# A transformer layer in FP32: right operands of the first FFN block made in reverse order, their sums a tile earlier, and another order of steps where the first attention ends

## The chip, the cores and the metric

The kernel runs on one core of one Trainium2 chip. The metric is the device time of one execution in microseconds (us). A core has these engines, each with a queue of its own that is worked off in order: PE (TensorE, matrix products; loading a stationary operand into it is listed apart as PEld), DVE (VectorE), ACT (ScalarE), POOL (GpSimd), and SP (SyncE), which here only issues DMAs. Matmul results land in PSUM banks, from which DVE and ACT read them; everything else lies in SBUF. Semaphores tie the engines together.

## The reference

One layer on 2048 rows of 576: attention with 32 query heads of 18 columns and one key/value head, then a bilinear feed-forward net (FFN) with 4608 hidden columns, each with a layernorm ahead of it and a residual sum behind it, all in FP32.

```python
q = (x @ wq).reshape(B, S, 32, 18);  k = x @ wk;  v = x @ wv
p = softmax(einsum("bhqd,bkd->bhqk", q, k) * 18 ** -0.5)
h = x + einsum("bhqk,bkd->bhqd", p, v).reshape(B, S, 576) @ wo     # x normalised ahead of q, k, v
g = n @ w_gate;  u = n @ w_up                                      # n: h normalised
out = h + (g * u) @ w_down
```

## The kernel before

**Blocks and tiles.** The 2048 rows are four blocks of 512 (b = 0 to 3). Matrix products keep FP32's accuracy by splitting an operand into a rounded part, hi (a cast), and the rest, lo (a difference, source minus hi), and summing three products: hi hi, hi lo, lo hi. `split` (line 86) does this with a copy on ACT, DVE or POOL and the difference on DVE (line 89).

**Attention** is done in pairs. `pair` (456) issues, for two heads and 128 keys, the scores on PE (`s`, line 476) and the exponential on ACT (`P`, 477). Two pairs make one step of `acc` (481), the product with the values, which `flush` (484) issues later. 32 pairs make a head group of four heads; eight groups make a block, so 256 pairs a block and 1024 in all. With a group's last step DVE transposes `acc` into `os` (492), and a step is put on the list `aux`: `normalise` (506), which divides by the sums, transposes back (523 to 528) and spreads the heads' rows over `ob` with DMAs (537). When enough heads are there, `chunk` splits their rows, and `project` (590) multiplies them with `wo` on PE (`yo`, 605) and adds the result to the residual on DVE (606). `run_aux` (496) takes due steps off `aux`, by default one a call; a call is a round.

**The order is written out by hand.** Block b+1's attention runs inside block b's FFN. Ahead of that, `blocks` (936) ends the first block's attention: first the splits of `wo` (until pair WO_FROM = 228), then the flag, then pairs and projections in turn, in which `fill` (864) issues about one pair for each 1.05 us that it is given. Then comes the layernorm: `normal` (631) makes `xh` on DVE and POOL, and `spread` (641) transposes it on PE (`tx`, 654) and splits it into `X`. It takes the pairs as far as a count that leaves 4 when divided by 8, and four more.

**The flag** (372) tells whether a bound on the scores is passed anywhere; if so, everything is computed a second time at the end with exact maxima. It takes a maximum on DVE, transposes it on PE (379) and compares on DVE.

**FFN.** `ffn` (791) goes through 36 tiles f of 128 hidden columns. A tile has 27 steps j, each with one matmul for `pg` and one for `pu` (811); while attention is left, a pair is issued at every fourth j and one behind the last, 8 a tile. ACT copies `pg` to `g` (835) and DVE multiplies `pu` by it, `hf` (839), which frees the PSUM banks of `pg` and `pu` for the next tile and, in even tiles, for `down`. Weights come by `load_w` (DMA `wr`) and `split_w` (POOL casts, DVE subtracts, `ws`), a tile ahead. Two tiles make a pair of halves p (0 to 17), which `down` (717) multiplies with `w_down` at the end of the next even tile: 42 matmuls `y` (771), using seven right operands in the order 0, 3, 4, 2, 5, 6, 1 (`ORDER`, 1032); this is a Strassen-like scheme with seven products in place of eight. DVE (774) or ACT and POOL (778, 779, over five buffers `tmp`) add the results to the residual.

**Right operands.** In block 0 they are made: `load_raw` (882) brings the four quarters of `w_down` for p, `right_sums` (889) makes three sums on POOL (891), `right` (902) makes one more sum (914), and for each operand a cast on POOL (915), a difference on DVE (918) and a DMA to HBM (921), from where blocks 1 to 3 load them. All these tiles have the tag `wdo`, ten buffers used in turn, as many as one p needs: two raw, one for sums, seven operands. Both run in odd tiles: the sums at j = 4, an operand at every odd j from 7 on. The last p (17) has no sums and four plain operands.

Of the kernel before, what the change touches and what calls it, by code (L numbers as in the profile page):

```python
# [17 lines left out]
F32 = mybir.dt.float32  # L18
# [7 lines left out]
P = 128  # L26
# [5 lines left out]
NG = H // 4  # L32
NF = F // P
NC = NF // 2
HT = TB // 2
HD = D // 2
# [22 lines left out]
class Block:  # L59
# [424 lines left out]
    def flush(self, n):  # L484

        for b, g, t, Ps in self.pend[:n]:
            if t == 0:
                self.acc = self.ps_a(f"acc{b}_{g}")
            self.values(self.acc, Ps, t)
            if t == NT - 1:  # L490
                os_ = self.os[g] = self.op.tile([P, TB], F32, tag="os", bufs=1, name=f"os{b}_{g}")
                self.dve.transpose(os_, self.acc)
                self.aux.append((self.round + 1, lambda b=b, g=g, o=os_: self.normalise(b, g, o), None))
        del self.pend[:n]

    def run_aux(self, limit=1, within=False):
# [93 lines left out]
    def project(self, b, c):  # L590

        pe, dve = self.pe, self.dve
        h, to = self.h[b], self.heads_to(b, c)
        w = self.wos.pop(c) if b else self.wo_0[0:rows(b, c), :, c]
        for s in range(NQ):
            sl = slice(s * P, (s + 1) * P)
            for n in range(2):
                y = self.ps_y(2 * s + n, f"yo{b}_{c}_{s}_{n}")
                d = slice(n * HD, (n + 1) * HD)
                if c < 4 or b == 0:  # L600
                    ms = [(to[0][:, sl], w[:, 0, d]), (to[1][:, sl], w[:, 0, d]), (to[0][:, sl], w[:, 1, d])]
                else:
                    ms = [(to[0][:, sl], w[:, 0, d]), (to[0][:, sl], w[:, 1, d])]
                for i, (m, k) in enumerate(ms):
                    pe.matmul(y[:, :HD], m, k, start=(i == 0), stop=(i == len(ms) - 1))  # L605
                dve.tensor_tensor(h[:, s, d], h[:, s, d], y[:, :HD], ALU.add)
            if b == 0:
                if c == 4:
                    self.statistics(b, s)
                if s % 2:  # L610
                    self.fill(2.4)
        if c == 3 and b:
            self.aux.append((self.round, lambda: self.chunk(b, 4), None))
        if c == 4:
            if b == 0:
                self.normed[b] = self.mv, self.rstd(self.mv[:, :, 1], f"b{b}")
            else:
                self.aux.append((self.round, lambda: self.all_statistics(b), None))
# [172 lines left out]
    def ffn(self, b):  # L791
        pe, act, dve = self.pe, self.act, self.dve
        X, hid, todo = self.X, [], None
        for f in range(NF):
            n_ = NF * b + f
            k = f % 2
            w = self.ws.pop(n_)
            on = self.more(b + 2)
            last = f == NF - 1 and b + 1 < NB
            if on:  # L800
                pg, pu = self.ps_f(f"pg{n_}"), self.ps_f(f"pu{n_}")
            else:
                gu = self.ps_s(f"gu{n_}")
                pg, pu = gu[:, 0], gu[:, 1]
            j = 0
            for c in range(9):
                for wk, xk in ((0, 0), (0, 1), (1, 0)):
                    if on and not last and j % 4 == 0 and self.more(b + 2):
                        self.pair()
                    for o, ps in ((0, pg), (64, pu)):  # L810
                        pe.matmul(ps, w[o:o + 64, wk, c], X[o:o + 64, xk, c], start=(j == 0), stop=(j == 26))  # L811
                    if j == (8 if on else 2) and todo and not plain(n_ - 2):
                        self.left_sums()
                    if j == 3:
                        self.split_w(n_ + 1)
                    if j == 5 and k:
                        self.left_first(n_ - 1, hid[0])
                    if j == 12:
                        self.run_aux(within=True)
                    if b == 0 and k and self.first:  # L820
                        if j == 4:
                            self.right_sums(f // 2)
                            parts = self.right(f // 2)
                        elif j > 6 and j % 2:
                            next(parts, None)
                    if j == 21 and b == f == 0:
                        self.flush(len(self.pend))
                    if j == 6 and last:
                        self.normal(b + 1)
                    j += 1  # L830
            if todo and not on:
                drain(self.down(b, *todo))
                self.more_wd(b, 7)
            g = self.hh.tile([P, TB], F32, tag="g", bufs=1, name=f"g{n_}")
            act.copy(g, pg)  # L835
            if on and not last and self.more(b + 2):
                self.pair()
            hf = self.hh.tile([P, TB], F32, tag="hf", bufs=2, name=f"hf{n_}")
            dve.tensor_tensor(hf, pu, g, ALU.mult)  # L839
            hid.append(hf)  # L840
            if k:
                self.left(n_ - 1, hid)
                hid = []
            self.flush(len(self.pend))
            if todo and on:
                drain(self.down(b, *todo))
                self.more_wd(b, 7)
            if f < NF - 1:
                self.run_aux()
            todo = (f // 2,) if k else None  # L850
        if b + 1 < NB:
            both(self.spread(b + 1), self.down(b, *todo))
            self.more_wd(b + 1, WD_BUFS if b == 0 and self.first else 4)
            if b + 2 < NB:
                self.load_x(b + 2)
        else:
            drain(self.down(b, *todo))
# [31 lines left out]
    def right_sums(self, p):  # L889

        sub = lambda o, x, y: self.nc.gpsimd.tensor_tensor(o, x, y, ALU.subtract)
        a, b = self.raw
        s = self.src = {0: a[:, 0], 1: a[:, 1], 2: b[:, 0], 3: b[:, 1]}
        if p == NC - 1:
            return
        r = self.wp.tile([P, 2, HD], F32, tag="wdo", bufs=WD_BUFS, name=f"sums{p}")
        s[4], s[5], s[6], s[7] = r[:, 0], r[:, 1], s.pop(0), r[:, 0]
        sub(s[4], s[6], s[1])
        sub(s[5], s[3], s[4])
        sub(s[6], s[3], s[6])  # L900

    def right(self, p):

        pool, dve, sp = self.nc.gpsimd, self.dve, self.sp
        s, ws, order = self.src, {}, range(4) if p == NC - 1 else ORDER
        o = 0 if p == NC - 1 else 1
        steps = list(order)
        self.raw = None
        for k in range(len(steps) + 2):
            if k < len(steps):  # L910
                j = steps[k]
                w = ws[j] = self.wdo[0, p, j] = self.wp.tile([P, 2, HD], F32R, tag="wdo", bufs=WD_BUFS, name=f"wdo0_{p}_{j}")
                if o and j == 6:
                    pool.tensor_tensor(s[7], s[2], s[5], ALU.subtract)
                pool.tensor_copy(w[:, 0], s[j + o])  # L915
            if 0 < k <= len(steps):
                j = steps[k - 1]
                dve.tensor_tensor(ws[j][:, 1], s[j + o], f32(ws[j][:, 0]), ALU.subtract)  # L918
            if k > 1:
                j = steps[k - 2]  # L920
                sp.dma_start(self.wd_dram[p, :, j], f32(ws.pop(j)))
            yield
        del s
        self.src = None
        self.load_raw(p + 1)
# [10 lines left out]
    def blocks(self):  # L936

        work = self.load_wo_0()
        self.steps(lambda: self.n_pair < WO_FROM, work)
        drain(work)  # L940
        self.wo_from = WO_FROM + 12
        if self.first:
            work = self.flag()
            self.steps(lambda: self.n_pair < WO_FROM + 8, work)
            drain(work)
        self.cast = self.dve.tensor_copy
        self.steps(lambda: self.more(0))
        self.cast = self.act.copy
        self.load_w(0)
        self.load_w(1)  # L950
        self.fill(2.0, 1)
        while 0 not in self.normed:
            self.run_aux(1)
            self.fill(1.0, 1)
        self.split_w(0)
        while self.n_pair % 8 != 4:
            self.pair()
            if not self.half:
# [73 lines left out]
ORDER = (0, 3, 4, 2, 5, 6, 1)  # L1032
WD_BUFS = 10
LANDING = 6
WO_FROM = 228
# [15 lines left out]
def plain(n):  # L1051

    return n % NF == NF - 2
# [6 lines left out]
def f32(ap):  # L1060
    return ap.bitcast(F32)
# [10 lines left out]
def rows(b, c):  # L1072

    return 7 * DH if b == 0 and c < 4 else P


def drain(gen):
    for _ in gen:
        pass
# [78 lines left out]
```

## Time and profile before

| | |
|---|---|
| median of 3 runs | 2346.53 us (2346.36 to 2346.98) |
| the profiled execution | 2345.53 us |
| its span, first to last instruction | 2343.7 us |
| TensorE clock granted, mean over the span | 0.995 |
| PE / PEld / DVE / ACT / POOL busy | 98% / 69% / 52% / 61% / 29% |
| chain that ended last, by engine | PE 88%, DVE 4%, POOL 3%, issue 2%, ACT 1%, DMA 1% |

The profile is of one execution. A row of a timeline has the start in us from the span's start, the duration in us (from the first to the end of the last where `xN` are merged), engine, operation, tiles written <- read, shapes, and in brackets the engine's idle time ahead of it with what ended it. A row of groups has count, busy time in us, mean ns of one, then idle time ahead and its releasers. A row of stretches has the busy time in us of PE, PEld, DVE, ACT and POOL with the number of instructions, then the granted clock, the share of the DMA engines and GB/s. Rows of the chain have start, duration, engine, tile and line. A matmul's duration overlaps its neighbour's, so PE is read by distances between starts.

### The profile page before, as it was taken

The page shows a single profiled execution, that of the slowest core. Times are in us where ns is not written, and L with a number is a line of the kernel's source. Part 1 is how long each engine was busy: PE and PEld are TensorE (multiplying, and loading weights), DVE is VectorE, ACT ScalarE, POOL GpSimd, SP SyncE. Part 2 cuts the span into 40 slices and gives each one's busy share as a digit, 9 for nine tenths or more (in the row PEclk, how much of TensorE's full clock was granted, in tenths as well). Part 3 has the DMA queues.
Part 4 walks back from the last instruction along what each step waited for, and adds up shares of the span by engine and source line. Part 5 has one row for each costly group of instructions (what it writes and reads, how often), then busy time and mean ns, then how long its engine had stood idle before and what let it go on. Part 6 is the DMA issues. An engine that isn't in the chain of part 4 may idle for free.

```text
span 2343.7 us, 46343 instructions
## 1 busy us (share of the span) xinstructions
PE 2292.6 (98%) x18225; PEld 1605.7 (69%) x18225; DVE 1207.9 (52%) x2174; ACT 1431.9 (61%) x1869; POOL 673.1 (29%) x873
## 2 busy tenths in 40 slices
PE   5999999999999999999999999999999999999998
PEld 4344434676767667777767767767777788888887
DVE  7333334566656566444444445534444476555665
ACT  4888876766666766567676767567676623223332
POOL 3100000455444345222222212312222234333332
PEclk9999999999999999999999999999999999999999
DMA  4222222443334443633433333544333345655553
GB/s 142 70 65 84 72 79 72 145 148 130 126 117 143 142 137 134 205 127 122 127 118 108 117 118 122 154 157 123 114 122 119 111 145 190 203 183 176 168 179 117
DMA packets 127225, 306.59 MB, mean 131 GB/s; under 512 B 15679, under 2 KB 16447, under 8 KB 126999
## 3 DMA queue, kind: packets, MB, share of 16 engines
q1 hardware_dynamic: 126999, 303.54, 39.9%
q8 instruction: 146, 2.39, 0.4%
q14 instruction: 80, 0.66, 0.1%
HBM read 234.00 MB, written 55.67 MB: 124 GB/s over the span
## 4 chain that ended last, share of the span: by engine, by line
PE 88%; DVE 4%; POOL 3%; issue 2%; ACT 1%; DMA 1%; SPq 0%; POOLq 0%; ACTq 0%; DVEq 0%
PE acc L481 19%; PE y L771 16%; PE pg L811 13%; PE s L476 12%; PE gu L811 12%; PE pu L811 10%; PE yo L605 3%; PE psq L331 3%; POOL wdo L915 1%; DVE wdo L918 1%; PE y L729 1%; ACT P L477 1%; POOL ws L88 0%; POOL x L779 0%; DVE hf L839 0%
## 5 line engine op out<-in xcount | busy, mean ns | idle before, releaser
L477 ACT ACTIVATE P<-s 128x1024 f32<-128x1024 f32 x1024 | 1024.6, 1027 | 291.0 <-PE s L476 211.6
L811 PE MATMUL pu<-X,ws 64*128 64x512 f32 x2565 | 699.8, 391 | 4.1 <-DVE hf L839 4.1
L811 PE MATMUL pg<-X,ws 64*128 64x512 f32 x2565 | 701.5, 391 | 0.0
L811 PEld LDWEIGHTS pg<-X,ws 64*128 64x128 f32 x2565 | 475.8, 186 | 53.6 <-DMA wr<-in_wgu_dram 0.8
L811 PEld LDWEIGHTS pu<-X,ws 64*128 64x128 f32 x2565 | 472.8, 186 | 46.2 <-DVE hf L839 7.1
L481 PE MATMUL acc<-P,V 128*32 128x512 f32 x4096 | 492.2, 600 | 1.1 <-ACT P L477 0.6
L476 PE MATMUL s<-q,kT 56*128 56x512 f32 x2048 | 443.0, 424 | 4.0 <-ACT P L477 3.3
L771 PEld LDWEIGHTS y<-wdo,room 128*128 128x128 f32 x2856 | 386.6, 188 | 52.8 <-issue 42.5
L771 PE MATMUL y<-wdo,room 128*128 128x288 f32 x2856 | 407.2, 301 | 2.3 <-DVE h L774 2.3
L778 ACT COPY tmp<-y 128x288 f32<-128x288 f32 x408 | 162.9, 400 | 328.8 <-PE y L771 323.8
L476 PEld LDWEIGHTS s<-q,kT 56*128 56x128 f32 x2048 | 198.3, 185 | 207.0 <-ACT P L477 119.8
L779 POOL TENSOR_TENSOR x<-x,tmp 128x288 f32<-128x288 f32 x204 | 159.2, 811 | 568.6 <-ACT tmp L778 566.9
L811 PE MATMUL gu<-X,ws 64*128 64x512 f32 x2646 | 308.1, 389 | 0.2
L811 PEld LDWEIGHTS gu<-X,ws 64*128 64x128 f32 x2646 | 256.0, 184 | 45.7 <-issue 4.0
L481 PEld LDWEIGHTS acc<-P,V 128*32 128x32 f32 x4096 | 114.5, 109 | 250.1 <-issue 233.0
L88 POOL CAST ws<-wr 128x1152 fp32r<-128x1152 f32 x144 | 169.1, 1174 | 354.9 <-PE gu L811 110.2
L779 POOL TENSOR_TENSOR h<-h,tmp 128x288 f32<-128x288 f32 x204 | 159.4, 812 | 341.7 <-ACT tmp L778 341.1
L89 DVE TENSOR_TENSOR ws<-wr,ws 128x1152 fp32r<-128x1152 f32 x144 | 204.2, 1418 | 77.5 <-POOL ws L88 77.5
L839 DVE TENSOR_TENSOR hf<-pu,g 128x512 f32<-128x512 f32 x95 | 65.5, 690 | 269.7 <-ACT g L835 269.7
L774 DVE TENSOR_TENSOR x<-x,y 128x288 f32<-128x288 f32 x272 | 117.4, 453 | 153.1 <-PE y L771 153.1
L774 DVE TENSOR_TENSOR h<-h,y 128x288 f32<-128x288 f32 x272 | 117.4, 453 | 93.0 <-PE y L771 90.2
L89 DVE TENSOR_TENSOR room<-S,room 128x1024 fp32r<-128x1024 f32 x68 | 83.3, 1225 | 132.3 <-ACT room L88 132.3
(169 smaller groups left out, 1729.3 us busy)
## 6 DMA issues: line engine op xcount, KB each, us to landing
wdo<-wd_dram SPq DMA_DIRECT2D x369, 288.0 KB
wr<-in_wgu_dram SPq DMA_DIRECT2D x144, 576.0 KB
wd_dram<-wdo SPq DMA_DIRECT2D x123, 288.0 KB
q<-q_dram SPq DMA_DIRECT2D x64, 216.0 KB
raw<-in_wd_dram SPq DMA_DIRECT2D x36, 288.0 KB
q_dram<-qs SPq DMA_DIRECT2D x16, 504.0 KB
X<-X SPq DMA_DIRECT2D x28, 256.0 KB
x<-in_x_dram SPq DMA_DIRECT2D x16, 288.0 KB
```

What stands on the lines that cost most here:

```text
L88: (copy or self.cast)(hi, src)
L89: self.dve.tensor_tensor(lo, src, f32(hi), ALU.subtract)
L331: pe.matmul(ps[:r], w[o:o + 64], m[o:o + 64], start=(k == 0), stop=(k == 13))
L476: self.pe.matmul(s_[:, i], self.kT[o:o + 56, t * P:(t + 1) * P], q[o:o + 56, pr], start=True, stop=True)
L477: self.act.activation(p_, s_, AF.Exp, scale=SCALE)
L481: self.pe.matmul(acc[32 * j:32 * j + 32, :], self.V[:, t, :], Ps[j // 2][:, j % 2, :], start=(t == 0), stop=(t == NT - 1), skip_group_chec ...
L605: pe.matmul(y[:, :HD], m, k, start=(i == 0), stop=(i == len(ms) - 1))
L771: pe.matmul(y[:, :HD], m[:, t * P:(t + 1) * P], k, start=(first and j == 0), stop=(j == 2), skip_group_check=True)
L774: dve.tensor_tensor(hs, hs, y[:, :HD], ALU.add)
L778: act.copy(z, y[:, :HD])
L779: pool.tensor_tensor(hs, hs, z, ALU.add)
L811: pe.matmul(ps, w[o:o + 64, wk, c], X[o:o + 64, xk, c], start=(j == 0), stop=(j == 26))
```

## The change

In `flush`, block 0's last group is normalised at once instead of through `aux`. In `project`, `fill` gets 2.1 instead of 2.4. In `blocks`, projections may begin at pair WO_FROM + 8 instead of + 12, the flag's steps are gone, the first two weight loads come at pair 228 and the first weight split ahead of the end of the pairs, and `run_aux` may take two steps a round while it waits for the layernorm. In `ffn`, block 0's even tiles make the three sums (one at each odd j from 9 on), its odd tiles make the operands from j = 7 on as before, and the flag's two parts stand in tiles 2 and 3 at j = 16. The operands are made in the order 1, 5, 2, 6, 4, 3, 0 (the last p, 17, with its plain ones: 3, 2, 1, 0), and the fourth sum is written over a raw quarter instead of over the first sum.

```diff
@@ flush
-                self.aux.append((self.round + 1, lambda b=b, g=g, o=os_: self.normalise(b, g, o), None))
+                if b == 0 and g == NG - 1:
+                    self.normalise(b, g, os_)
+                else:
+                    self.aux.append((self.round + 1, lambda b=b, g=g, o=os_: self.normalise(b, g, o), None))
@@ project
-                    self.fill(2.4)
+                    self.fill(2.1)
@@ ffn
-                    if b == 0 and k and self.first:
-                        if j == 4:
-                            self.right_sums(f // 2)
-                            parts = self.right(f // 2)
-                        elif j > 6 and j % 2:
+                    if b == 0 and self.first:
+                        if j == (6 if k else 8):
+                            parts = self.right(f // 2) if k else self.right_sums(f // 2)
+                        if j % 2 and j > (6 if k else 8):
                             next(parts, None)
+                        if j == 16 and f in (2, 3):
+                            flag = self.flag() if f == 2 else flag
+                            next(flag, None)
@@ right_sums
-        if p == NC - 1:
-            return
-        r = self.wp.tile([P, 2, HD], F32, tag="wdo", bufs=WD_BUFS, name=f"sums{p}")
-        s[4], s[5], s[6], s[7] = r[:, 0], r[:, 1], s.pop(0), r[:, 0]
-        sub(s[4], s[6], s[1])
-        sub(s[5], s[3], s[4])
-        sub(s[6], s[3], s[6])
+        self.raw = None
+        if p < NC - 1:
+            r = self.wp.tile([P, 2, HD], F32, tag="wdo", bufs=WD_BUFS, name=f"sums{p}")
+            s[4], s[5], s[6], s[7] = r[:, 0], r[:, 1], s.pop(0), s[2]
+            for i, x, y in ((4, 6, 1), (5, 3, 4), (6, 3, 6)):
+                sub(s[i], s[x], s[y])
+                yield
@@ right
-        s, ws, order = self.src, {}, range(4) if p == NC - 1 else ORDER
-        o = 0 if p == NC - 1 else 1
-        steps = list(order)
-        self.raw = None
+        s, ws, o = self.src, {}, int(p < NC - 1)
+        steps = (1, 5, 2, 6, 4, 3, 0) if o else (3, 2, 1, 0)
@@ blocks
-        self.wo_from = WO_FROM + 12
-        if self.first:
-            work = self.flag()
-            self.steps(lambda: self.n_pair < WO_FROM + 8, work)
-            drain(work)
+        self.wo_from = WO_FROM + 8
+        self.load_w(0)
+        self.load_w(1)
         self.cast = self.dve.tensor_copy
+        self.steps(lambda: self.n_pair < WO_FROM + 8)
+        self.split_w(0)
         self.steps(lambda: self.more(0))
         self.cast = self.act.copy
-        self.load_w(0)
-        self.load_w(1)
         self.fill(2.0, 1)
         while 0 not in self.normed:
-            self.run_aux(1)
+            self.run_aux(2)
             self.fill(1.0, 1)
-        self.split_w(0)
```

## The prediction

> **What bounds the kernel now.** I read the page first, then the busy times of three stretches of equal meaning, then the chain of waits.
>
> ```profile
> span 2343.7 us, 46343 instructions
> PE 2292.6 (98%) x18225; PEld 1605.7 (69%) x18225; DVE 1207.9 (52%) x2174; ACT 1431.9 (61%) x1869; POOL 673.1 (29%) x873
> ...
> core 0: us, PE busy (x) PEld busy (x) DVE busy (x) ACT busy (x) POOL busy (x), PEclk, DMA share, GB/s
> 323.20:402.05 78.85, 71.63 (x462) 32.89 (x463) 38.20 (x94) 53.73 (x58) 6.76 (x9) 0.96 0.16 46
> ...
> 439.50:944.90 505.40, 500.44 (x4052) 354.25 (x4048) 312.40 (x531) 338.51 (x437) 237.27 (x309) 1.00 0.40 136
> 1004.05:1496.40 492.35, 492.15 (x4052) 350.22 (x4048) 227.68 (x419) 339.36 (x437) 115.70 (x133) 1.00 0.38 120
> ...
> 500.90 6.11 PE y L771 x42
> ...
> 1037.23 5.83 PE y L771 x42
> 1066.91 5.82 PE y L771 x42
> ```
>
> TensorE sets the time, so only what makes it wait or run slowly can be won. Two places have such time. The end of the first attention (323 to 402 us) leaves it idle for 78.85 - 71.63 = 7.2 us and at 0.96 of its clock. FFN block 0 (its 16 downs from 439.5 to 944.9) does the same 4052 matmuls as block 1 does from 1004.05 to 1496.40, in 505.40 instead of 492.35 us: 13.05 us more. Block 0 differs by making the right operands on POOL and DVE. The chain gives one part: a down's 42 matmuls take 6.11 us there and 5.83 in block 1, 0.28 x 16 = 4.5 us. The other 8.6 lie in the tiles, and the timeline of one pair of tiles shows where:
>
> ```profile
> 477.28 0.82 POOL L891 TENSOR_TENSOR sums<-raw 128x288 f32<-128x288 f32 x1
> 478.18 1.80 POOL L891 TENSOR_TENSOR sums<-raw,sums 128x288 f32<-128x288 f32 x1
> 479.95 0.99 POOL L891 TENSOR_TENSOR raw<-raw,raw 128x288 f32<-128x288 f32 x1
> 480.88 0.43 POOL L915 CAST wdo<-raw 128x288 fp32r<-128x288 f32 x1
> ...
> 481.34 0.65 DVE L918 TENSOR_TENSOR wdo<-raw,wdo 128x288 fp32r<-128x288 f32 x1 [1.07 <-POOL wdo L915]
> ...
> 482.51 0.39 DVE L523 TENSOR_SCALAR rc<-os 128x16 f32<-128x16 f32 x1
> ...
> 485.00 1.38 DVE L918 TENSOR_TENSOR wdo<-sums,wdo 128x288 fp32r<-128x288 f32 x1
> ...
> 487.87 0.44 DVE L918 TENSOR_TENSOR wdo<-raw,wdo 128x288 fp32r<-128x288 f32 x1
> 488.24 0.67 DVE L839 TENSOR_TENSOR hf<-pu,g 128x512 f32<-128x512 f32 x1
> ...
> 483.95 0.58 ACT L835 COPY g<-pg 128x512 f32<-128x512 f32 x1
> 488.97 0.50 PE L811 MATMUL pu<-X,ws 64*128 64x512 f32 x1 [0.80 <-DVE hf L839]
> ```
>
> This is tile 5. POOL's three sums hold its casts up until 480.88, DVE waits 1.07 us for the first cast, then works without a break, with the normalise of a head group in between (482.5 to 485.0), until hf at 488.24, though g was there at 484.53. PE needs hf, since it frees pu's bank, and stands still. So the chain of this place is POOL sums, POOL casts, DVE differences, hf, PE.
>
> **The change, part by part.** *The flag leaves the attention.* These are PE's rows about it:
>
> ```profile
> 321.61 1.07 PE L481 MATMUL acc<-P,V 128*32 128x512 f32 x8
> ...
> 325.62 1.07 PE L481 MATMUL acc<-P,V 128*32 128x512 f32 x8
> 328.99 0.20 PE L379 MATMUL psx<-C,mx 32*1 32x32 f32 x1 [2.30 <-DVE mx L376]
> 329.12 1.22 PE L476 MATMUL s<-q,kT 56*128 56x512 f32 x4
> 330.28 1.94 PE L481 MATMUL acc<-P,V 128*32 128x512 f32 x8
> ...
> 338.17 1.87 PE L605 MATMUL yo<-wo,oT 126*128 126x288 f32 x12
> ...
> 320.00:340.00 20.00, 16.78 (x99) 5.56 (x91) 8.97 (x16) 14.41 (x16) 5.83 (x6) 0.83 0.42 134
> ```
>
> Four pairs take 4.01 us (321.61 to 325.62). The eight from 325.62 to the first project at 338.17 take 12.55 instead of 8.0: 4.5 us for the flag, of which 2.30 is the wait of its transpose for DVE's maximum and the rest matmuls at a lower granted clock (0.83 in this slice; eight acc records 1.94 us instead of 1.07). In the tiles the maximum stands a whole tile ahead of its transpose, so nothing waits; PE pays the 0.20 us matmul and a weight load, DVE three small operations in tiles with slack. I put 0.3 us there (bounds 0.2, the matmul alone, and 2.5, the same wait again).
>
> [...]
>
> *Projections from pair 236 instead of 240, normalise of the last group at once, two aux steps a round, fill 2.1.* I counted the order on PE along the code (S one pair, A one acc step, Y one s of a project). Between the first and the fourth project before and after both have 12 Y, 22 S and 12 A, so the 31.40 us from 338.17 to 369.57 stay. The first project begins four pairs earlier and without the flag: 12.55 becomes 4.0, minus 8.5 us. From the fourth project to the first gate matmul it was YYSSYYSSASSAA, YYSSSYYSASSAASSAASS, then transposes and SSAA; it becomes YYSSYYSSAS, YYSASYYSASSAAASS and the same end, four pairs fewer.
>
> ```profile
> 369.57 1.45 PE L605 MATMUL yo<-wo,oT 126*128 126x288 f32 x9
> 371.32 0.67 PE L605 MATMUL yo<-wo,oT 126*128 126x288 f32 x3 [0.30 <-DVE x L606]
> 380.03 1.74 PE L605 MATMUL yo<-wo,oT 128*128 128x288 f32 x11 [0.31 <-DVE oT L89]
> 394.82 2.40 PE L654 MATMUL tx<-C,xh 128*128 128x128 f32 x20 [0.94 <-ACT P L477]
> ...
> 365.40 0.72 DVE L492 STREAM_TRANSPOSE os<-acc 128x512 f32<-128x512 f32 x1 [2.09 <-PE acc L481]
> ...
> 390.28 1.36 DVE L89 TENSOR_TENSOR ws<-wr,ws 128x1152 fp32r<-128x1152 f32 x1
> ...
> L477 ACT ACTIVATE P<-s 128x1024 f32<-128x1024 f32 x280 | 272.3, 1024 | 72.1 <-PE s L476 71.2 <-ACT P L477 0.3
> ...
> 2184.64 0.69 DVE L839 TENSOR_TENSOR hf<-gu,g 128x512 f32<-128x512 f32 x1 [3.37 <-ACT g L835]
> 2202.93 0.69 DVE L839 TENSOR_TENSOR hf<-gu,g 128x512 f32<-128x512 f32 x1 [3.36 <-ACT g L835]
> ```
>
> Leg one (9.8 us, to the fifth project at 379.35) loses S, A, A = 2.2 us of PE work, but DVE's transpose (0.72) and normalise (about 1.7) now stand directly ahead of the fourth project's adds, so the wait of 0.30 becomes some 1.5, and the last chunk has one S of cover instead of SSAA, so 0.31 becomes some 1.5 (two P of about 1.0 us, the cast and the difference, against 2.0 us of PE work): 9.8 - 2.2 + 1.2 + 1.2 = about 10, of which I take 9.3, since the waits overlap PE's own slack. Leg two (15.5 us, to the transposes at 394.82) loses three S, 1.0 us, and the ws difference (1.36 us at 390.28) leaves DVE's chain from the last project to xh, which ends it: 12.6. The end, 394.82 to 402.05, stays. Together 32.5 becomes about 29.0, minus 3.5 (bounds plus 1, if both waits come on top, and minus 6). The early weight loads and split_w(0) stand on SP and POOL behind the wo splits, ahead of the ob copies of group 6, which are needed 25 us later; DVE's 1.36 us lie between adds where PE has pairs: nothing.
>
> The eight pairs are not saved. Before, 280 P stand ahead of the first tile, after it 272, and FFN block 2 does the eight later. Their price there: two tiles with 16 pairs take 29.68 us (1037.23 to 1066.91), without 18.29 (2184.64 to 2202.93), so 0.71 each, 5.7 us. The end of the attention is worth -8.5 - 3.5 + 5.7 = -6.3 us (bounds -2 and -9).
>
> *Sums in the even tile.* With 272 pairs at the start and 8 a tile, a group of 32 ends after an odd tile, so normalise moves from odd tiles to even ones. The odd tile loses 3.6 us of POOL (477.28 to 480.88) ahead of the casts, DVE's wait of 1.07, and normalise's 2.5 us of DVE. DVE starts its seven differences at about 480.3 and needs 0.44 to 0.65 each: done by 485, against 488.24. PE's wait ends if hf comes 1.0 us earlier, so it goes, in the tiles with normalise and in the others. Of the 8.6 us I take 8.0 (bounds 4, if only the tiles without normalise gain, and 8.6). The sums themselves move to a stretch in which POOL is idle:
>
> ```profile
> 494.86 0.91 SPq L887 DMA_DIRECT2D raw<-in_wd_dram  x2
> ...
> 498.04 0.69 DVE L839 TENSOR_TENSOR hf<-pu,g 128x512 f32<-128x512 f32 x1 [2.34 <-ACT g L835]
> 502.85 4.73 POOL L779 TENSOR_TENSOR x<-x,tmp 128x288 f32<-128x288 f32 x6 [15.95 <-ACT tmp L778]
> ...
> 501.00:502.00 1.00, 1.00 (x9) 1.00 (x9) 0.48 (x2) 0.00 (x0) 0.00 (x0) 1.00 0.00 0
> ```
>
> POOL has 15.95 idle us there and DVE 2.34 ahead of hf, and even a late hf has until 500.8, where the down needs the bank. raw has landed by 501 (no DMA runs after it) and is issued earlier with DVE ahead. So I put the sums at nothing; without that cover they would cost their 2.4 us a down.
>
> [...]
>
> *Reverse order.* Today the operand used first is made first, so at each later operand's first use PE has to wait anew for POOL's count. Made last, its one wait covers all seven, as POOL finishes in order. The 0.28 us that a down is slower than in block 1, which has no such waits, is the nearest row; I take all of it, 4.5 us (bounds 0 and 5). The new tile for s[7] is raw's own, read before it is overwritten: nothing.
>
> Sum: -6.3 + 0.3 - 8.0 - 4.5 = -18.5 us, on the profiled execution (2345.53 us, 1.8 around the span) 2327.0; the median of the runs is 1.0 above that execution, so 2328.0. Tile edges of blocks 0 and 2, whose parity turns too, may add or take 1.5.
>
> **The rivals.** [...] *The order does nothing:* the slower down comes from DVE's evictions, and 4.5 stay: 2332.5. *The clock falls again* at the two new waits of 1.5 us, some six apart: behind the flag the slow rows cost 4.5 - 2.3 = 2.2 us where PE had slack left, perhaps half as much again here where it has little, 3.4: 2331.4. For it speaks that 2.30 us sufficed once; against it, that waits of 1 us in tile 5 did not. *POOL waits for raw*, and this one is slower: the sums stand in POOL's queue ahead of the down's adds, and tmp has five buffers, so ACT's sixth eviction (506.2) waits for the first add. With raw at R that add ends at R + 2.4 + 0.8; from R = 503 on each down waits, break-even is 1.16 us a down (18.5 / 16), R = 504.2, and R = 504.6 costs 1.6 x 16 = 25 us: 2353. Against it: the DMA queues are empty by 501. *Nothing moves*, because the pairs return at full price and another wait takes hf's place: 2346.5.
>
> **How the numbers follow.** Forecast 0.58 (its own range 2323 to 2332), DVE holds hf 0.12, order does nothing 0.10, clock 0.06, POOL waits 0.11, nothing 0.03. The measurement can tell about 0.2%, 4.7 us, from no change: faster 0.86, same 0.03, slower 0.11. The range goes from 2322 (all gains at their upper bounds) to 2339 (hf held and the end of the attention at its lower bound).
>
> **What would show it.** No wait of PE for hf in block 0 and no DVE wait for the first cast; 16 downs in about 493 us; a down of 5.8 us; no psx wait and a clock of 1.0 from 320 to 340; 272 P ahead of the first tile, whose first gate matmul comes near 390. I am wrong if the odd tile's hf still comes after 487 in its place, if POOL's adds wait for sums, if y stays at 6.1, or if a slice ahead of 390 shows a lower clock.

## The result, and the profile after

| | median of the runs | lowest to highest | runs |
|---|---|---|---|
| before | 2346.54 us | 2345.64 to 2348.36 | 20 |
| after | 2343.09 us | 2341.31 to 2345.31 | 20 |

The ratio of after to before is 0.9985, with an interval from 0.9978 to 0.9992: the changed kernel is a little faster, by 3.5 us instead of the 18.5 that were forecast. The time lies outside the predicted range.

The page of the profile shows how little is left of the gain; PE was 2292.6 us busy and is 2283.8:

```profile
span 2340.6 us, 46187 instructions
PE 2283.8 (98%) x18225; PEld 1602.6 (68%) x18225; DVE 1210.6 (52%) x2175; ACT 1433.3 (61%) x1868; POOL 684.0 (29%) x873
```

To see where the time went, both spans are cut at the same points of the work. A good mark is `hf`, which is made once a tile. First the stretches of the kernel before, then those of the one after; the first stretch of each runs from the first `hf` to the `hf` of tile 33 of block 0, the second on to the first `hf` of block 1, the third to tile 22 of block 2, the fourth to its tile 29.

```profile
413.71:930.05 516.34, 511.03 (x4134) 361.22 (x4134) 314.77 (x521) 347.26 (x447) 245.68 (x322) 1.00 0.40 134
930.05:977.36 47.31, 46.24 (x372) 35.51 (x368) 28.29 (x62) 26.59 (x36) 14.81 (x22) 1.00 0.62 196
977.36:1860.77 883.41, 882.34 (x7258) 625.90 (x7254) 397.47 (x716) 605.55 (x777) 202.49 (x236) 1.00 0.40 126
1860.77:1942.10 81.33, 78.41 (x622) 65.75 (x616) 56.36 (x119) 22.21 (x44) 28.59 (x34) 1.00 0.50 164
```

```profile
401.22:908.45 507.23, 503.47 (x4135) 354.73 (x4135) 311.90 (x511) 349.96 (x448) 255.29 (x319) 1.00 0.41 138
908.45:963.36 54.91, 49.20 (x372) 38.65 (x368) 33.34 (x76) 25.70 (x35) 14.38 (x21) 0.97 0.50 156
963.36:1846.52 883.16, 882.05 (x7258) 627.33 (x7254) 396.10 (x716) 605.76 (x777) 201.55 (x236) 1.00 0.40 126
1846.52:1938.28 91.76, 85.21 (x670) 70.26 (x664) 57.18 (x118) 29.97 (x52) 28.89 (x34) 0.98 0.47 145
```

| stretch | before | after | difference |
|---|---|---|---|
| start to the first `hf` | 413.71 | 401.22 | -12.5 |
| block 0, tiles 0 to 33 | 516.34 | 507.23 | -9.1 |
| tile 33 to block 1 | 47.31 | 54.91 | +7.6 |
| block 1, and block 2 to tile 22 | 883.41 | 883.16 | -0.3 |
| block 2, tiles 22 to 29 | 81.33 | 91.76 | +10.4 |
| the rest | 401.60 | 402.32 | +0.7 |

The differences add up to -3.1, the difference of the spans. The gain of the first two stretches, 21.6 us, is there; 18.7 are given back in three places. Of these the forecast had put down only 5.7, for the eight pairs that block 2 now does. The stretch from tile 33 to block 1 also shows it in its own columns after the change: PE is idle for 54.91 - 49.20 = 5.7 us of it, before for 1.1, and the granted clock is 0.97 instead of 1.00.

**What went as planned.** A stretch of the kernel after, in which the kernel before had a granted clock of 0.83, and then rows of the timeline about the end of the first attention, the downs and tile 5:

```profile
320.00:340.00 20.00, 19.19 (x132) 8.89 (x124) 13.07 (x22) 16.35 (x18) 5.82 (x6) 1.00 0.51 166
```

```profile
363.41 0.67 PE L608 MATMUL yo<-wo,oT 126*128 126x288 f32 x3 [1.52 <-DVE x L609]
369.62 0.37 PE L608 MATMUL yo<-wo,oT 128*128 128x288 f32 x1 [0.82 <-issue]
370.30 1.75 PE L608 MATMUL yo<-wo,oT 128*128 128x288 f32 x11 [0.31 <-DVE oT L89]
389.54 0.39 PE L814 MATMUL pg<-X,ws 64*128 64x512 f32 x1
...
427.03 5.90 PE L774 MATMUL y<-wdo,room 128*128 128x288 f32 x42
926.26 5.93 PE L774 MATMUL y<-wdo,room 128*128 128x288 f32 x42
...
471.30 0.45 DVE L921 TENSOR_TENSOR wdo<-raw,wdo 128x288 fp32r<-128x288 f32 x1
472.19 0.69 DVE L844 TENSOR_TENSOR hf<-pu,g 128x512 f32<-128x512 f32 x1 [0.44 <-ACT g L840]
```

The clock is full from 320 to 340, the first gate matmul starts at 389.54 instead of 402.05, and in tile 5 the differences are done before `hf` can begin: `hf` waits 0.44 us for ACT's `g` and no longer for DVE's own earlier work. Sixteen downs take 926.26 - 427.03 = 499.2 us instead of 505.4, and each is 0.2 us shorter (5.90 and 5.93 against 6.11). Counted between the starts of its first and its last matmul, a down took 5.88 us before and takes 5.62 (medians), as much as in block 1 before, 5.61.

**What is new: projections behind odd tiles.** The first attention now ends at 272 pairs. A group of 32 pairs is then full behind an odd tile (288 pairs behind tile 1), its normalise comes in the even tile, and its projection `yo` behind the next odd one, where it used to stand behind an even one. The timeline of PE and DVE at such a place, then the group of the `yo` over block 0's downs with its waits, after (L608) and before (L605):

```profile
501.16 3.64 PE L481 MATMUL acc<-P,V 128*32 128x512 f32 x32
504.73 1.45 PE L608 MATMUL yo<-wos,room 128*128 128x288 f32 x9
507.06 2.27 PE L608 MATMUL yo<-wos,room 128*128 128x288 f32 x15 [0.88 <-DVE x L609]
...
503.77 0.68 DVE L844 TENSOR_TENSOR hf<-pu,g 128x512 f32<-128x512 f32 x1
504.49 0.42 DVE L711 TENSOR_TENSOR S<-hf,hf 128x256 f32<-128x256 f32 x1
...
505.96 0.69 DVE L89 TENSOR_TENSOR room<-hf,room 128x512 fp32r<-128x512 f32 x1
506.56 3.26 DVE L609 TENSOR_TENSOR x<-x,yo 128x288 f32<-128x288 f32 x8
```

```profile
L608 PE MATMUL yo<-wos,room 128*128 128x288 f32 x112 | 18.0, 308 | 5.2 <-DVE x L609 5.2
...
L605 PE MATMUL yo<-wos,room 128*128 128x288 f32 x112 | 17.7, 304 | 0.9 <-DVE x L774 0.7
```

PE issues nine matmuls, three results, and then needs a bank that DVE empties. But behind an odd tile DVE first has `hf`, the four S sums of the pair's left operands and a difference, and starts the adds of `yo` only at 506.56. PE stands still for 0.88 us, although 3.64 us of `acc` stood ahead of `yo`. Five such waits are 5.2 us, against 0.9 before: four of 0.83 to 0.88 us, and one of 1.82 us at 912.35, which lies behind tile 33 and so in the stretch to block 1.

**The last projection of block 0 comes a tile later,** and with it the layernorm's statistics. The timeline at block 0's end, and two stretches of 3.5 us:

```profile
932.60 0.81 DVE L103 BATCH_NORM_STATS2 bsb<-x 128x6 f32<-128x288 f32 x2
...
938.66 0.16 DVE L125 SCALAR_TENSOR_TENSOR yb<-tb,yb 128x4 f32<-128x4 f32 x1
938.74 1.36 DVE L89 TENSOR_TENSOR ws<-wr,ws 128x1152 fp32r<-128x1152 f32 x1
...
940.61 2.04 DVE L640 TENSOR_SCALAR xh<-x,mvb,yb 128x576 f32<-128x576 f32 x4
...
938.14 0.61 PE L814 MATMUL pu<-X,ws 64*128 64x512 f32 x2
941.82 0.33 PE L657 MATMUL tx<-C,xh 128*128 128x128 f32 x1 [3.07 <-POOL xh L641]
```

```profile
938.30:941.80 3.50, 0.45 (x3) 0.03 (x1) 3.43 (x8) 0.59 (x1) 0.45 (x1) 1.00 0.19 39
942.50:946.00 3.50, 3.34 (x16) 3.11 (x16) 2.73 (x6) 0.00 (x0) 2.41 (x6) 0.51 0.44 168
```

Statistics and their root (932.60 to 938.8) now stand on DVE directly ahead of `xh`, which is needed for block 1's transposes. PE waits 3.07 us, and the clock is then at 0.51 for 3.5 us. With the 1.82 us of the late projection this is the better part of the 7.6 us.

**The same two things at the end of block 2,** where the eight missing pairs are also done. No pairs are left there in the last tiles, so no `acc` covers the projections, which now stand behind odd tiles here too. Rows of PE's timeline, and two stretches:

```profile
1889.72 2.27 PE L608 MATMUL yo<-wos,room 128*128 128x288 f32 x15 [2.63 <-DVE h L609]
...
1914.54 2.51 PE L608 MATMUL yo<-wos,room 128*128 128x288 f32 x10 [3.03 <-DVE h L609]
...
1926.50 4.73 PE L774 MATMUL y<-wdo,room 128*128 128x288 f32 x33 [0.89 <-DVE h L777]
```

```profile
1889.70:1893.20 3.50, 3.48 (x27) 3.10 (x29) 3.48 (x8) 0.71 (x2) 0.00 (x0) 1.00 0.02 5
...
1915.00:1919.00 4.00, 4.00 (x19) 3.32 (x20) 3.77 (x8) 0.00 (x0) 0.00 (x0) 0.57 0.00 0
```

The waits are 2.63, 3.03 and 0.89 us, and behind the second of them the clock is at 0.57. PE is idle for 91.76 - 85.21 = 6.55 us of the stretch from tile 22 to 29, before for 2.92. So of the 10.4 us that the stretch is longer, 3.6 are idle time and 6.8 are more busy time, in which the eight pairs (5.7 by the forecast) and the slow clock lie.

### The profile page after: what moved, and what is told of

Same layout as the page of the kernel before. It is cut to its first block, busy times and chain, and to the rows that moved or that the text cites. A ratio compares the mean times of both kernels' runs of the same rounds, so it can differ in the third digit from the quotient of the medians.

```text
span 2340.6 us, 46187 instructions
## 1 busy us (share of the span) xinstructions
PE 2283.8 (98%) x18225; PEld 1602.6 (68%) x18225; DVE 1210.6 (52%) x2175; ACT 1433.3 (61%) x1868; POOL 684.0 (29%) x873
## 4 chain that ended last, share of the span: by engine, by line
## 5 line engine op out<-in xcount | busy, mean ns | idle before, releaser
L814 PE MATMUL pu<-X,ws 64*128 64x512 f32 x2592 | 707.0, 391 | 0.0
L814 PEld LDWEIGHTS pg<-X,ws 64*128 64x128 f32 x2592 | 481.4, 186 | 58.9 <-issue 1.2
L814 PEld LDWEIGHTS pu<-X,ws 64*128 64x128 f32 x2592 | 478.5, 186 | 36.7 <-DMA X<-X 0.4
L476 PE MATMUL s<-q,kT 56*128 56x512 f32 x2048 | 436.8, 422 | 2.5 <-ACT P L477 1.8
L814 PE MATMUL gu<-X,ws 64*128 64x512 f32 x2592 | 303.1, 390 | 0.0
L814 PEld LDWEIGHTS gu<-X,ws 64*128 64x128 f32 x2592 | 248.9, 185 | 48.0 <-issue 5.2
```

Source lines behind the costliest of these rows:

```text
L476: self.pe.matmul(s_[:, i], self.kT[o:o + 56, t * P:(t + 1) * P], q[o:o + 56, pr], start=True, stop=True)
```

## The experiments

The theory after the result was: the three gains are real, and what eats them is that groups of heads, and so projections, now end behind odd tiles. The remedy would be to turn this parity (whether groups end behind odd or even tiles) back by doing the eight pairs ahead of the first tile again.

**e1_eight_more: the changed kernel with 280 pairs ahead of the first tile.**

```diff
-        while self.n_pair % 8 != 4:
+        while self.n_pair < 276:
```

> The changed kernel with eight more pairs ahead of the first FFN tile (280 instead of 272), so that head groups again end behind even tiles. Theory (turned tiles: what was won until tile 33 of block 0 is given back because the projections and the statistics of the next block fall a tile later): the first tile starts about 8 us later than in the changed kernel, block 0's 16 downs take 493 to 496 us instead of 499.2, the 3.07 us wait of the transposes for xh in the last tile is gone, block 2's end loses no more than before; 2331 us (2328 to 2334). Rival A (the sums in the even tiles cost at the block's end wherever the groups end): the loss in tiles 34 and 35 stays, 2338 to 2341. Rival B (the eight moved pairs cost 10 us in block 2 and not 5.7): only that comes back, minus 10 plus 8, 2341.

Measured: 2344.15 us, ratio 0.9989 (0.9980 to 0.9998). The theory missed: no time is won. The tile edges behave nearly as before the change (the stretch to block 1 takes 48.66 us, the end of block 2 81.23), but block 0 became slow instead: 517.06 us from tile 0 to 33, where the changed kernel needs 507.23. The group of `y` names the new wait:

```profile
L774 PE MATMUL y<-wdo,room 128*128 128x288 f32 x2856 | 407.4, 301 | 10.3 <-DVE hf L844 8.1 <-DVE h L777 2.2
```

PE waits 8.1 us for `hf` ahead of downs. Something in even tiles is late; what it is shows in e4.

**e2_flag_only: the kernel before, with the flag in tiles 2 and 3.**

```diff
+                    if b == 0 and self.first and j == 16 and f in (2, 3):
+                        flag = self.flag() if f == 2 else flag
+                        next(flag, None)
...
-            work = self.flag()
-            self.steps(lambda: self.n_pair < WO_FROM + 8, work)
-            drain(work)
+            self.steps(lambda: self.n_pair < WO_FROM + 8)
```

> The kernel before with the flag alone moved into tiles 2 and 3 and nothing else. Theory: the transpose's wait and the slow clock behind it go, 4.5 us, and the tiles pay 0.3: 2342.3 us (2341 to 2343.5), clock 1.0 from 320 to 340 us. Rival: the wait or the lower clock turns up at the next gap of the attention's end: 2345 to 2346.5.

Measured: 2343.04 us against 2346.60, ratio 0.9985 (0.9976 to 0.9994): minus 3.6. The flag's move is worth what the whole change brings.

**e4_sums_and_order: the kernel before, with the change's sums in the even tile and its reverse order,** its own end of the attention and 280 pairs.

```diff
+                    if b == 0 and self.first:
+                        if j == (6 if k else 8):
+                            parts = self.right(f // 2) if k else self.right_sums(f // 2)
+                        if j % 2 and j > (6 if k else 8):
+                            next(parts, None)
...
+        steps = (1, 5, 2, 6, 4, 3, 0) if o else (3, 2, 1, 0)
```

> The kernel before with the sums in the even tiles and the operands in reverse order of use, and its own end of the attention, flag and 280 pairs. Theory: 8.0 us for hf in time and 4.5 us for the shorter downs, nothing given back at the block's end as groups end behind even tiles: 2334 us (2332 to 2337), 16 downs in 493 to 495 us. Rival (DVE, not POOL, holds hf in the tiles with normalise): the downs give 4.5 and the tiles without normalise 2.5: 2339 to 2341.

Measured: 2346.68 us, ratio 1.0001 (0.9992 to 1.0010): nothing, as in e1 and against the expectation. Four downs wait for `hf`, 0.99, 1.06, 1.92 and 4.14 us. The timeline of the longest wait, at the end of tile 30, an even one, tells why, with one stretch behind it. SPq is SP's DMA queue:

```profile
870.01 1.61 SPq L886 DMA_DIRECT2D raw<-in_wd_dram  x2
...
875.10 0.79 POOL L890 TENSOR_TENSOR sums<-raw 128x288 f32<-128x288 f32 x1 [15.16 <-DMA raw<-in_wd_dram]
...
876.70 0.66 POOL L88 CAST wos<-wor 128x576 fp32r<-128x576 f32 x1
...
877.40 1.33 DVE L89 TENSOR_TENSOR wos<-wor,wos 128x576 fp32r<-128x576 f32 x1 [9.01 <-POOL wos L88]
878.65 0.68 DVE L838 TENSOR_TENSOR hf<-pu,g 128x512 f32<-128x512 f32 x1
...
879.39 6.90 PE L771 MATMUL y<-wdo,room 128*128 128x288 f32 x33 [4.14 <-DVE hf L838]
```

```profile
877.50:884.40 6.90, 5.01 (x21) 5.02 (x22) 3.30 (x6) 1.60 (x4) 3.34 (x5) 0.51 0.00 0
```

`raw` is issued only at 870.01. The sum at the head of POOL's queue waits for it until 875.10, and the cast of the next projection's `wos`, which has nothing to do with `raw`, stands behind. DVE's difference of `wos` waits 9.01 us for that cast, `hf` stands behind the difference, and the down waits 4.14 us for `hf`. The clock is then 0.51 for 6.9 us. With 280 pairs the `wos` splits fall in even tiles, where the sums now are. With 272 they fall in odd ones, so the changed kernel's sums also wait for `raw` (75.8 us in 15 waits over block 0's downs, as in the row below), but no matmul of `y` waits there. It has turned the parity, and pays for it elsewhere.

```profile
477.97 0.81 POOL L896 TENSOR_TENSOR sums<-raw 128x288 f32<-128x288 f32 x1 [5.22 <-DMA raw<-in_wd_dram]
```

**e8_sums_behind_wos: e1 with the sums from j = 15 of the even tile on,** behind the cast of `wos` in POOL's queue.

```diff
-                        if j == (6 if k else 8):
+                        if j == (6 if k else 14):
-                        if j % 2 and j > (6 if k else 8):
+                        if j % 2 and j > (6 if k else 14):
-        while self.n_pair % 8 != 4:
+        while self.n_pair < 276:
```

> As the changed kernel with eight more pairs (280, groups end behind even tiles), and the sums of the even tile from j = 15 on instead of 9, so that on POOL the cast of the wo slice (j = 12) stands ahead of them. Theory (where groups end behind even tiles, the sums wait for raw ahead of that cast, DVE waits for the cast ahead of hf, and the down waits for hf): the four waits of the downs of 0.8 to 4.0 us and the slow clock behind two of them go, 11 us less than with eight pairs alone: 2333 us (2331 to 2336), 16 downs in 493 to 495 us. Rival (it is DVE's own load where normalise and the differences share an odd tile): waits of about 0.8 us for hf come back in the gate matmuls, 2338 to 2341.

Measured: 2330.58 us (2329.69 to 2330.75) against 2345.61, ratio 0.9934 (0.9921 to 0.9948), a little below the expected range. Against e1 (ratio 0.9989), which differs in the place of the sums alone, some 13 us are won. The first and the last of its downs, then the projection behind tile 6, an even one, and DVE's first add of its results:

```profile
436.15 5.91 PE L774 MATMUL y<-wdo,room 128*128 128x288 f32 x42
930.19 5.91 PE L774 MATMUL y<-wdo,room 128*128 128x288 f32 x42
...
501.93 3.79 PE L608 MATMUL yo<-wos,room 128*128 128x288 f32 x24
502.53 0.45 DVE L609 TENSOR_TENSOR x<-x,yo 128x288 f32<-128x288 f32 x1
```

Sixteen downs take 494.0 us, and DVE takes the results of `yo` from 502.53 on, 0.6 us behind the first matmul, with no sums ahead of them; PE does not wait. The forecast for the change, 2328.0, was in reach; it needed both the parity of before and later sums.

**e9_old_end: the kernel before with flag, late sums and reverse order;** of the change it leaves out the other order of steps at the attention's end.

> The kernel before with the flag in tiles 2 and 3, the sums from j = 15 of the even tiles on and the reverse order; its own end of the attention apart from the flag (280 pairs, projections from pair 240, fill 2.4, normalise through the list). Theory (apart from the flag the other order of steps is worth nothing once the eight pairs are back): as the version with the sums behind the wo cast to within 1 us, 2333 to 2334. Rival (the other order gains 3 us of its own): 2336 to 2337, 3 us slower than that version.

Measured: 2329.96 us (2329.29 to 2332.30), ratio 0.9933 (0.9920 to 0.9947), 3 us below the expected number. Within the scatter this is e8, as was expected. So beside the flag, the other order of steps at the attention's end is worth nothing once the eight pairs are done there again.

**e10_sums_alone: the kernel before with the late sums only,** in the old order of operands and with its own flag.

> The kernel before with the sums alone moved into the even tiles, from j = 15 on; old order of making, own end with flag. Theory: hf comes in time in all odd tiles, PE's waits for hf (7 of 0.3 to 0.8 us, 8 us with what follows) go, downs stay at 5.87: 2338.5 us (2337.5 to 2340). Rival (normalise keeps hf late in every second odd tile): four of the waits of 0.8 stay, 2341 to 2343.

Measured: 2337.83 us, ratio 0.9965 (0.9952 to 0.9979): minus 7.8. **e7_order_only: the kernel before with the reverse order only.**

```diff
-        s[4], s[5], s[6], s[7] = r[:, 0], r[:, 1], s.pop(0), r[:, 0]
+        s[4], s[5], s[6], s[7] = r[:, 0], r[:, 1], s.pop(0), s[2]
...
+        s, ws, o = self.src, {}, int(p < NC - 1)
+        steps = (1, 5, 2, 6, 4, 3, 0) if o else (3, 2, 1, 0)
```

> The kernel before with the reverse order of making alone; sums in the odd tile as before. Theory (each operand's first use brings PE a new wait for POOL's count when the first used is made first): a down of 42 matmuls takes 5.6 us from first to last start instead of 5.87, in 17 downs 4.5 us: 2342 us. Rival (the downs are slow by DVE's evictions beside the differences): 5.87 stays, 2346.5.

Measured: 2344.12 us against 2345.61, ratio 0.9992 (0.9983 to 1.0001): minus 1.5, 2 us less than expected, and not told from no change. The groups of PE between 439 and 945 us, first of e10, then of e7:

```profile
L811 PE MATMUL pu<-X,ws 64*128 64x512 f32 x867 | 237.1, 391 | 0.0
L771 PE MATMUL y<-wdo,room 128*128 128x288 f32 x714 | 104.8, 305 | 0.0
```

```profile
L811 PE MATMUL pu<-X,ws 64*128 64x512 f32 x864 | 237.2, 392 | 5.1 <-DVE hf L839 5.1
L771 PE MATMUL y<-wdo,room 128*128 128x288 f32 x684 | 96.7, 300 | 0.0
```

The two edits do different things. Late sums end every wait of `pu` for `hf`, and a matmul of `y` keeps its 305 ns. The reverse order brings that to 300 ns, but 5.1 us of waits for `hf` stay, where the kernel before has 4.1. Between the starts of its first and last matmul a down takes 5.64 us in e7, as was expected, and 5.88 in e10 and before. The single starts say where the time goes. Before and in e10, four starts of a down come some 200 ns behind the one ahead of them, where most come about 132: each right behind the first matmul that uses operand 4, 5, 6 or 1. In e7 and the changed kernel these four are 137 to 173 ns (medians), about as in block 1 (145 to 155), where the operands are loaded. At all four the first PSUM bank is taken up again too, but that is so in every order; at the first use of operands 3 and 2 no such gap shows. In e9, which has both and the flag, 15.65 us are won; less 3.56 for the flag and 7.78 for the sums, 4.3 us are left for the order; 0.26 us in each of the 16 downs are 4.2.

**e5_stats_earlier and e13_stats_block1: the changed kernel with the last `wo` load brought forward,** so that the last projection and the statistics behind it come a tile earlier, in e5 for all blocks, in e13 for block 1 only (the diff is e13's).

```diff
-        if b and c == 4:
+        if b > 1 and c == 4:
             self.load_wo(c)
...
+            if c == 3 and 1 not in self.normed:
+                self.load_wo(4)
...
-                self.aux.append((self.round, lambda: self.all_statistics(b), None))
+                self.aux.append((self.round + (b == 1), lambda: self.all_statistics(b), None))
```

> The changed kernel with the last fifth of wo loaded a projection earlier, so that the last projection of a block's attention and the statistics behind it come one tile earlier; 272 pairs as in the changed kernel. Theory (turned tiles): the statistics no longer stand ahead of xh in block 0's last tile, the wait of 3.07 us and the slow clock behind it go, about 7 us; block 2's end gets back 2 to 5 us; the other projections stay at the ends of odd tiles with waits of 0.85 us; 2333 us (2330 to 2337). Rival A (the loss is not the statistics' place): 2343. Rival B (block 2 pays for the pairs): 2336, with block 2's end as slow as in the changed kernel.

> The changed kernel with the last fifth of wo loaded a projection earlier for block 1 alone, so that block 1's last projection falls into an even tile and its statistics ahead of tile 34; blocks 2 and 3 as in the changed kernel. Theory (statistics ahead of xh cost 3 us of waiting and the slow clock behind it, the last projection's wait 1.8): 5 to 7 us less than the changed kernel at the first tile of block 1, block 2's end as in the changed kernel: 2337 us (2335 to 2340). Rival (the loss moves to the next wait): 2341 to 2343.

Measured: e5 2339.77 us, ratio 0.9972 (0.9960 to 0.9984); e13 2336.42 us (2335.57 to 2338.41), ratio 0.9959 (0.9945 to 0.9973). In both the transposes no longer wait, as this row of e13 shows, which has no bracket:

```profile
937.19 2.40 PE L659 MATMUL tx<-C,xh 128*128 128x128 f32 x20
```

The stretch from tile 33 to block 1 takes 48.71 us in e13 instead of 54.91. So the late last projection and the statistics behind it, which the edit moves together, are the cause of that loss, about 6.2 us of the 7.6. In what is left PE is still slow for a while: behind waits of 0.84, 0.20 and 0.29 us 42 matmuls of `y` take 7.38 us, where the changed kernel takes 6.00 for the same 42 at a clock of 1.00. For block 2 the same edit does harm: e5 missed its expectation because the end of block 2, with new waits of up to 3.56 us, gave about half of it back.

**e11_sums_late: the changed kernel with the sums from j = 15,** its 272 pairs kept.

> The changed kernel (272 pairs) with the sums from j = 15 of the even tiles on; against the version with eight more pairs and the same late sums (2330.6 us) it differs by the eight pairs alone. Theory (with 272 pairs a group ends behind odd tiles and everything behind it comes a tile later: projections behind odd tiles, the statistics at the end of tile 34, block 2's last projections in tiles without pairs): as the changed kernel, 2343 us (2341 to 2345), 12 us above the version with 280. Rival (the place of the sums is what costs): 2330 to 2333, and the eight pairs are worth minus 3.

Measured: 2342.96 us, ratio 0.9986 (0.9977 to 0.9995): the same as the changed kernel. It differs from e8 in the eight pairs alone, and is 12.4 us slower. Late sums by themselves bring the change nothing.

**e12_sixteen_more: e11 with 288 pairs ahead of the first tile,** so that groups still end behind odd tiles, as with 272.

```diff
-        while self.n_pair % 8 != 4:
+        while self.n_pair < 284:
```

> The version with late sums and sixteen more pairs than the changed kernel (288), so that groups end behind odd tiles as in the changed kernel, but everything of block 0's end comes a tile earlier than with 280. Pairs: plus 8.6 ahead, minus 5.7 in block 2. Theory (two separate costs, the odd tile's projections with 5 us in block 0 and 4.7 at block 2's end, and the late statistics with 7): the statistics do not meet xh, no 3 us wait ahead of the transposes, but the projections' waits are there: 2343 us (2340 to 2345). Rival A (lateness alone costs): 2333.5. Rival B (all that the changed kernel loses comes from groups ending behind odd tiles, statistics too): 2347.

Measured: 2348.01 us (2345.17 to 2350.28), ratio 1.0009 (1.0000 to 1.0018). The waits of `yo` behind odd tiles are there again, 0.83 to 1.39 us each, and so are waits of 2.62 and 3.03 us at block 2's end: these go with the parity. The loss at block 0's end is not there (tile 33 to block 1 in 47.78 us): it goes with 272, by which the last projection of block 1's attention meets the layernorm. The time missed the expectation by 5 us and lies near rival B's 2347, though the statistics, which rival B counts in, cost nothing here. Part of it shows in the stretches: block 0 up to tile 33 takes 514.45 us (505.02 in e8), and block 2 up to tile 29 takes 414.47 (413.76 in e8), although eight pairs fewer are left for it.

## Why the prediction was wrong

**The flag: right.** -4.5 + 0.3 = -4.2 us were put down; e2 gave -3.6.

**The end of the attention: right up to the first tile, wrong behind it.** The start was to come 8.5 + 3.5 = 12.0 us earlier and came 12.5 us earlier. The legs fit too: leg one took 9.2 us (9.3 forecast), leg two 12.7 (12.6). Of the two new waits of "some 1.5" the first came as worked out, 1.52; at the second the wait for DVE's difference stayed at 0.31, with 0.82 us ahead of it for which the trace shows no releaser.

**The step that failed** is the price of the eight pairs that are put off. The text has them return in block 2 for 5.7 us and counts the turned parity of the tiles only with "Tile edges of blocks 0 and 2, whose parity turns too, may add or take 1.5". The parity was seen, and its gain was taken: normalise leaves the odd tile. But each group has three steps, and the other two move as well. The projection moves behind odd tiles, where DVE has the S sums ahead of it; block 1's last projection and statistics move up against `xh`. At the start the forecast gained 12.0 us, of which 4.5 were the flag's; the other 7.5 less 5.7 made putting the pairs off a gain of 1.8. e11 against e8, which differ in them alone, shows a loss of 12.4. In the stretches: after against e8 gains 9.1 at the first `hf` (401.22 against 410.32) and loses 2.2 in block 0 (505.02 in e8), 7.6 at its end (47.35), 10.5 at the end of block 2 (81.28) and about 1 behind it. Against its own sum the forecast is short by 15.4 us: 7.6 at block 0's end and 10.4 - 5.7 = 4.7 at block 2's, for which the sum had nothing, 3.1 in block 0 up to tile 33 (-9.1 where -8.0 - 4.5 + 0.3 = -12.2 were put down), while the rest cancels. Four waits of `yo`, 3.4 us, lie in that part of block 0.

**The sums: right in size, and by luck harmless.** -8.0 was put down, e10 gave -7.8, with no wait of `pu` left. That they cost nothing in the even tile because `raw` "has landed by 501" looked only at the end of the tile. The sums stand in POOL's queue from the middle of the tile on and wait there, and what stands behind them waits too. The rival *POOL waits for raw* had the right wait, 15.16 us in e4, but looked at the adds and `tmp` behind the sums, and not at the cast of `wos`. In the changed kernel this cast is in odd tiles; in e1 and e4, with 280 pairs, the waits for `hf` (8.1 us ahead of downs in each) and the slow clock behind them (0.51 for 6.9 us behind the longest in e4) eat the gain.

**The reverse order: right within its bounds.** -4.5 was put down (bounds 0 and 5). The starts of the matmuls give 16 x 0.26 = 4.2, e9 4.3 as the remainder; e7 by itself won 1.5, with 1.0 us more of waits for `hf`. The reason given, a new wait at each later operand's first use, fits four of the six such places, where the time is won; no row names the wait itself. By the trace, 96 semaphore instructions of 51 ns stand among the weight loads of block 0's sixteen downs before the change and none after it; in block 1 before there are 96 too, with downs of 5.61 us.

**The sixteen downs** were forecast at 493 us and took 499.2; the 5.2 us of `yo` waits are the better part of this. e8 and e9 have 494.0 and 493.9.

**The other rivals.** *DVE holds hf* fell: in tile 5 `hf` waits 0.44 us for ACT's `g`, and e10, the late sums alone, won 7.8 of the 8.0 us that were to stay. *The order does nothing* fell: e7 has DVE's evictions as before, and its downs are shorter. *The clock falls again* was right in that the clock fell, but at neither of the places named: the two waits of the attention's end left it at 1.00, and it fell at 942.5 (0.51 over 3.5 us) and at 1915 (0.57 over 4 us), behind waits of 3.07 and 3.03 us that had not been foreseen.

Without the eight pairs the forecast's terms are -4.2 - 8.0 - 4.5 = -16.7, and they hold for a kernel that keeps 280 pairs and has the sums behind the cast: e9, with flag, late sums and order alone, won 15.65 us (2329.96). The version that beats both kernels is this one or e8.

## What to carry to other kernels

When a change shifts the phase of a repeated sequence, follow every later step of that sequence to its new place, and list on each engine what stands ahead of it there; the gain at the step one is looking at is only one of several. An instruction that is moved to an idle stretch of an engine's queue brings its wait along (15.16 us for `raw` in e4): ask who stands behind it in that queue, related or not (there the cast of `wos`, for which DVE waited 9.01 us). Sum up the parts alone as well as together: here flag and late sums are each a gain alone, the order shows its gain only beside them, and a fourth, eight pairs put off, cost 12 us.

## What the runs showed of the hardware

**A short wait of PE can be followed by half the clock.** Behind the 3.07 us at 941.82 the granted clock was 0.51 for 3.5 us, behind the 3.03 us at 1914.54 it was 0.57 over 4 us, and from within the 4.14 us in e4 on 0.51 for 6.9 us; behind the 2.63 us at 1889.72 it stayed at 1.00 until 1893.20. At half clock 0.57 over 4 us makes 3.4 us, 0.51 over 6.9 us makes 6.8, and the flag's 0.83 over 20 us about as much. Cut finer, the clock is 0.50 in every quarter of a microsecond from 942.75 to 945.75 and from 1915.50 to 1918.75 after the change, and in every half from 328.50 to 335.00 before it. An estimate from these: PE loses up to 1.7 us in a slow stretch of 3.4. PE need not have stood still throughout: it was busy for 0.45 of the 3.5 us ahead of 941.80 and had run until 938.75. How much waiting is enough no run here shows.

**The same wait may or may not be followed by slow matmuls.** At the end of block 0 PE waits 0.83 or 0.84 us for ACT in e1, e8, e9 and e13. The 144 matmuls of `y` in the first downs of blocks 1 to 3, of which 48 stand about this wait, take 305 ns each in e8, and 318, 318 and 317 in e1, e9 and e13; the 42 behind the wait take 7.32 us in e1 and 7.38 in e13. The stretch from tile 33 to block 1 takes 48.66 to 48.71 us in these three instead of the 47.35 of e8.
